# Two layers of linear attention and MLP on one core: the seven products of an MLP step in another order, with a planner that counts waits of a bank and the times of the DMA queue

## The chip, the cores and the metric

The kernel runs on one core of a Trainium2 chip. A core has five instruction streams that run side by side and meet through semaphores: TensorE (PE, matmuls and the weight loads ahead of them), VectorE (DVE), ScalarE (ACT), GpSimd (POOL) and SyncE (SP, which here issues every DMA). The metric is the device time of one execution, in microseconds (us); smaller is better. Before the change its median is 1041.44 us over three runs, from 1040.10 to 1042.91.

## What is computed

Two layers, each an attention block and an MLP block with a residual around each, on 2048 rows of 512 numbers:

```python
x = A_x
x = x + _A_ref(_layernorm(x, axis=-1), A_wqkv, A_w_phi, A_wo)
x = x + _B_ref(_layernorm(x, axis=-1), B_w1, B_w2)
x = x + _A_ref(_layernorm(x, axis=-1), A_wqkv, A_w_phi, A_wo)
x = x + _B_ref(_layernorm(x, axis=-1), B_w1, B_w2)
```

The attention block has 32 heads of 16. Queries and keys go through a learned 16x16 map per head and two softmaxes (of the result and of its negative, 32 features); the output is linear attention, `phi_q (phi_k^T V) / (phi_q phi_k^T 1)`, and a projection by `wo`. The MLP is `relu(x @ w1) @ w2` with 1792 hidden columns.

## The kernel before

**Numbers.** Every large matrix is held as a high and a low fp16 half, and a product is the sum of three matmuls (high by high, high by low, low by high). All of it accumulates in fp32 in PSUM.

**Stages.** The 2048 rows are 16 chunks of 128 rows. A first stage makes keys and values of all chunks and gathers `phi_k^T V` in two PSUM banks (`kv0`, `kv1`). The opening of a layer (`opening`, `summary`) turns these sums into the right-hand side `rhs` of the numerators (`pn`), brings chunks 0 and 1 through the back projection (`pw`) and computes the remaining queries (`pq`). Then the MLP runs over tiles of 256 rows (two chunks), each in 7 steps of 256 hidden columns; between the steps stand, as side work, the query features of later chunks (`look`), their numerators and back projection, and in layer 0 also keys, values and sums for layer 1.

**A step of the MLP.** In tiles 2 to 6 of layer 0 and 1 to 7 of layer 1, 84 steps in all, the 2x2 block product of a step is done in seven block products instead of eight (`hidden_by_seven`, PE line L1007). All seven go into one PSUM bank `ph` with four quarters of 128 columns, `at(0)` to `at(3)`. A running sum stands in `at(2)`: products 1, 6, 7 and 4 are added to it in this order, and after 1, 6 and 7 ACT copies it to SBUF (`snap`, L1019, tile `sn`). DVE then adds a copy to another quarter (`plus`, L1025): the first to product 2 in `at(0)`, the third to product 5 in `at(1)` giving `at(3)`, the second to `at(1)` once product 3 is there too. At the end ACT (L909) and DVE (L912) take the relu of the whole bank as two halves `h0` and `h1`, and the bank is free. Layer 0 has two banks for `ph`; in layer 1 `kv0` and `kv1` serve as well, so four take turns. The second half of the MLP (`mlp_out`, `py`, L1106) multiplies an earlier step's `h` by `w2`, in four pieces of three matmuls of 512 columns; LAG = 2 sets how many steps later.

**Which matmul is which in the profile.** `ph<-yT,w` is product 1 or 2, `ph<-wq_h,w` or `ph<-wq_l,w` product 4, `ph<-yT,s` product 3 or 7, `ph<-wq_h,s` or `ph<-wq_l,s` products 5 and 6 (`wq` holds sums of rows by then, `s` the sums of weights, loaded anew for each step by a DMA, L966). A product is 6 matmuls of 128 columns.

**What sets the order.** The order on each engine is made before the program is built. `add` records tasks with their engine, an assumed duration and what they read and write; `Plan.order` is a list scheduler that plays these through and issues whatever can start first. Block products and `py` pieces are moreover kept in the order of writing by `in_line`. Whoever reads or writes different quarters of a bank is independent for this planner. The framework that sets the semaphores, on the other hand, counts the whole bank: a product that is issued after a copy out of its bank waits for that copy, whatever quarter it writes, and a copy waits for the products issued before it. For a DMA the planner assumes a time in the queue and a landing (`t.kb` is its size). `NUDGES` is a table of numbers that shift tasks' ranks; ranks decide between tasks that could start at the same time.

**The order of a step before** (`steps_by_seven`; a dash marks products of the step ahead): 1, 4', 2, 3', side work, `py`, 6, 5, `py`, side work, 7, `py`, `py`.

## Time and profile before

| | before |
|---|---|
| device time, median of 3 (lowest, highest) | 1041.44 us (1040.10, 1042.91) |
| the profiled execution's own time | 1039.46 us |
| its span | 1037.7 us |
| PE busy | 992.8 us, 96% |
| DVE, ACT, POOL busy | 664.9, 495.3, 481.1 us |
| granted PE clock | 0.9 or more in 37 of 40 slices, 0.8 in the other three |

The span is the stretch between the first and the last instruction of one execution; the 1.8 us that the execution's time has more lie around it. Busy time of PE includes the drain of a matmul behind the last one of a run, so a short wait does not show as idle time. Rows of the timeline give the start of a run of equal instructions, its length, and in brackets the idle time before it with what ended it. PEld is the loading of the stationary operand, which runs ahead of the matmuls on the same instruction stream.

### The profile page before, as it was taken

What the parts mean: (1) busy time and instruction counts of PE and PEld (TensorE: products, weight loads), DVE (VectorE), ACT (ScalarE), POOL (GpSimd) and SP (SyncE); (2) the same over time, 40 slices, a digit from 0 to 9 for tenths busy, and PEclk for the clock granted to TensorE, in tenths of its full rate; (3) what the DMA queues carried; (4) which work ended last, traced back from release to release, by engine and by line L of the source; (5) the groups of instructions that cost most, each with busy time, mean ns of one, the idle gap of its engine ahead of it and who ended that gap; (6) DMA issues with size and microseconds to landing.
All of it is one profiled execution on the core that took longest, in us unless ns stands there. A gap on an engine that the chain in (4) does not pass through costs nothing.

```text
span 1037.7 us, 22144 instructions
## 1 busy us (share of the span) xinstructions
PE 992.8 (96%) x8930; PEld 626.5 (60%) x8930; DVE 664.9 (64%) x1391; ACT 495.3 (48%) x918; POOL 481.1 (46%) x389
## 2 busy tenths in 40 slices
PE   6999997899998999999999999999998999999998
PEld 5555554666665665657566664566665666676664
DVE  6778989884675867667565228987875444444332
ACT  7987875444534544435343215554554334333221
POOL 1379875479553645626342215357754323123000
PEclk9999998899999999999999999999999999999999
DMA  9576663466839383856743416674779384763531
GB/s 326 195 221 164 186 174 118 112 155 156 238 95 222 79 220 94 207 117 174 170 131 110 138 48 152 191 163 91 177 187 215 87 224 118 195 159 102 148 123 42
DMA packets 239143, 161.40 MB, mean 156 GB/s; under 512 B 178368, under 2 KB 185536, under 8 KB 239040
## 3 DMA queue, kind: packets, MB, share of 16 engines
q1 hardware_dynamic: 239040, 159.98, 59.3%
q8 instruction: 70, 1.15, 0.4%
q14 instruction: 33, 0.27, 0.1%
HBM read 88.64 MB, written 28.31 MB: 113 GB/s over the span
## 4 chain that ended last, share of the span: by engine, by line
PE 69%; DVE 12%; DMA 7%; ACT 5%; POOL 4%; issue 3%; SPq 1%; ACTq 0%; DVEq 0%; POOLq 0%
PE py L1106 22%; PE ph L1007 15%; PE pk L550 6%; PE ph L1075 6%; PE pw L550 6%; PE pv L550 5%; PE pq L550 5%; DMA pT<-p_q 2%; DMA yT<-n_b 2%; PE pn L802 2%; PE kv L688 2%; ACT sn L1019 1%; DMA xT<-n_a 1%; DVE fm_q L594 1%; DVE e_q L586 1%
## 5 line engine op out<-in xcount | busy, mean ns | idle before, releaser
L1106 PE MATMUL py<-w,h 128*128 128x512 f16 x1344 | 335.5, 380 | 0.0
L1106 PEld LDWEIGHTS <-h 128*128 128x128 f16 x1344 | 120.6, 98 | 97.8 <-issue 0.3
L1007 PEld LDWEIGHTS <-s 128*128 128x128 f16 x2016 | 129.9, 98 | 43.6 <-issue 9.7
L1019 ACT ACTIVATE sn<-ph 128x128 f32<-128x128 f32 x252 | 69.3, 275 | 177.2 <-PE ph L1007 172.6
L1025 DVE TENSOR_TENSOR ph<-ph,sn 128x128 f32<-128x128 f32 x252 | 70.9, 296 | 128.8 <-PE ph L1007 86.4
L550 PEld LDWEIGHTS <-xT 128*128 128x128 f16 x840 | 81.4, 98 | 95.8 <-issue 1.4
L912 DVE SCALAR_TENSOR_TENSOR h<-ph,h 128x512 f16<-128x512 f32 x112 | 76.1, 680 | 83.8 <-ACT h L909 83.8
L1007 PEld LDWEIGHTS <-w 128*128 128x128 f16 x1512 | 94.1, 98 | 38.5 <-issue 18.5
L909 ACT ACTIVATE h<-ph 128x512 f16<-128x512 f32 x112 | 66.3, 592 | 92.5 <-DVE ph L1025 63.0
L603 POOL TENSOR_TENSOR e_k<-e_k,fm_k 128x1024 f32<-128x1024 f32 x30 | 60.8, 2026 | 77.9 <-ACT fm_k L599 77.9
L1007 PE MATMUL ph<-yT,w 128*128 128x128 f16 x1008 | 83.3, 219 | 10.4 <-ACT sn L1019 6.4
L603 POOL TENSOR_TENSOR e_q<-e_q,fm_q 128x1024 f32<-128x1024 f32 x32 | 62.3, 1947 | 62.2 <-ACT fm_q L599 61.9
L1007 PE MATMUL ph<-yT,s 128*128 128x128 f16 x1008 | 83.9, 219 | 4.3 <-ACT sn L1019 2.9
L614 POOL TENSOR_TENSOR p_q<-e_q,p_q 128x1024 f16<-128x1024 f32 x32 | 71.5, 2237 | 35.0 <-ACT p_q L610 29.4
L550 PE MATMUL pw<-wo_h,oT 128*128 128x512 f16 x256 | 82.4, 384 | 2.2 <-DMA oT<-n_o 2.0
L550 PE MATMUL pv<-wv_h,xT 128*128 128x512 f16 x256 | 81.0, 379 | 0.7 <-DVE m_w L317 0.4
L550 PE MATMUL pk<-wk_h,xT 128*128 128x512 f16 x256 | 81.0, 379 | 0.1
L1075 PE MATMUL ph<-yT,w 128*128 128x256 f16 (+1 forms) x768 | 79.6, 264 | 0.2 <-DMA yT<-n_b 0.2
L469 POOL TENSOR_TENSOR n_o<-o,n_o 128x512 f16<-128x512 f32 x28 | 34.0, 1213 | 96.6 <-ACT n_o L466 96.6
L614 POOL TENSOR_TENSOR p_k<-e_k,p_k 128x1024 f16<-128x1024 f32 x30 | 68.3, 2276 | 20.3 <-ACT p_k L610 20.2
L1075 PEld LDWEIGHTS <-w 128*128 128x128 f16 x768 | 68.9, 100 | 9.8 <-issue 0.5
L550 PE MATMUL pq<-wq_h,xq 128*128 128x512 f16 x208 | 65.4, 379 | 0.4 <-ACT qs L711 0.4
(188 smaller groups left out, 1727.2 us busy)
## 6 DMA issues: line engine op xcount, KB each, us to landing
s<-s_dram SPq DMA_DIRECT2D x84, 512.0 KB, 4.0
q_dram<-qs SPq DMA_DIRECT2D x32, 256.0 KB, 3.1
ql<-q_dram SPq DMA_DIRECT2D x32, 256.0 KB, 3.3
xt_dram<-xT SPq DMA_DIRECT2D x26, 256.0 KB, 2.6
xq<-xt_dram SPq DMA_DIRECT2D x26, 256.0 KB, 3.1
xe<-in_A_x_dram SPq DMA_DIRECT2D x16, 256.0 KB, 5.7
x<-in_A_x_dram SPq DMA_DIRECT2D x16, 256.0 KB, 3.4
x_dram<-x SPq DMA_DIRECT2D x16, 256.0 KB, 2.7
```

Source lines behind the costliest of these rows:

```text
L469: add(POOL, 0.1 + n / 490, lambda: nc.gpsimd.tensor_sub(n16.at()[:, n:], src(), n16.at()[:, :n]), reads=[x], writes=[(n16, "l")])
L550: nc.tensor.matmul(pm.ap, xT.ap[:, a, k, :], W.ap[b][:, k, :], start=(k == 0 and i == 0), stop=(k == KC - 1 and i == 2))
L603: (nc.vector if fast else nc.gpsimd).tensor_tensor(e3, e3, sm.unsqueeze(2).to_broadcast([P, 2 * n, DH]), op=ALU.mult)
L614: (nc.vector if fast else nc.gpsimd).tensor_sub(p16.ap[:, 1, cols], ef, p16.ap[:, 0, cols])
L688: nc.tensor.matmul(o, k16.ap[:, a, g * P:(g + 1) * P], v.ap[:, b, g, :], start=(c == 0 and g % 4 == 0 and i == 0), stop=(c == NCH - 1 and ...
L909: nc.scalar.activation(h[0].ap, at(), AF.Relu)
L912: add(DVE, 0.62, lambda: nc.vector.scalar_tensor_tensor(h[1].ap, at(), 0.0, h[0].ap, op0=ALU.max, op1=ALU.subtract), reads=[ph, h[0]], wri ...
L1007: nc.tensor.matmul(at(r), weight_of(i, b, kk, s, summed), rows_of(y, i, a, kk), start=(first and kk == 0 and n == 0), stop=(kk == 1 and n ...
L1019: nc.scalar.activation(saved(i), at(2), AF.Copy)
L1025: add(DVE, 0.27, lambda: nc.vector.tensor_tensor(at(o), at(r), saved(i), op=ALU.add), reads=[(ph, r), (sn, i)], writes=[(ph, o)], boost=10 ...
L1075: nc.tensor.matmul(at()[:, j, cs.start * P:cs.stop * P], W1.at(b, k, slice(f * P, (f + 1) * P)), yT.ap[:, cs, a, k, :], stop=(k == KC - 1 ...
L1106: nc.tensor.matmul(py.ap, h[a].ap.rearrange("p j t -> p (j t)")[:, cols], W2.at(b, fs[j], slice(0, D)), start=(s == j == k == 0), stop=(s ...
```

## The change

The seven products are issued in another order. After the change a step reads: 1, 4', `py`, 3', 2', side work, 5, 6, `py`, side work, `py`, 7, `py`. Product 2 thus moves to the end of its step, behind product 3, and with it its `plus`; the two additions that end a step now stand one after the other ahead of the relu.

In the planner, a product now also depends on all earlier uses of its bank, the time assumed for a product is 0.336 instead of 0.34, and the queue of DMAs is modelled otherwise: a transfer takes its size by 190 or 250 KB per us in the queue (190 for a DMA transpose) instead of 1000 or 330. `NUDGES` is another table. So the order of nearly everything else moves as well; the operations themselves, their number and their sizes stay. Lines behind the table of nudges come two or three lines later in the changed file.

```diff
 NUDGES = (
-    (0, 995, (40000006, 40000018, 40000194, 40000198, 40000434, 40000986, 40001073, 40003344, 40003700, 40004317,
...
+    (0, 995, (10000087, 10000443, 10000979, 10001562, 10002629, 10003322, 10003862, 10004370, 10004598, 10005107,
...
             if t.engine == SP:
-                queue = max(t.end, queue) + t.kb / (1000 if t.turn else 330)
-                t.end = queue + (1.8 if t.turn else 2.2)
+                queue = max(start + (1.2 if t.turn else 0.85), queue) + t.kb / (190 if t.turn else 250)
+                t.end = queue + (0.45 if t.turn else 0.8)
...
-            in_line(add(PE, 0.34, go, reads=[op, *(W1.res if i in (1, 2, 4) else [summed])],
-                        makes=[ph] if first else [], writes=[] if first else [(ph, r)]))
+            in_line(add(PE, 0.336, go, reads=[op, *(W1.res if i in (1, 2, 4) else [summed])],
+                        makes=[ph] if first else [], writes=[] if first else [(ph, r)],
+                        after=[] if first else [u for u, _, _ in ph.uses]))
...
-        def second():
-            product(2, 0)
-            plus(0, 0, 0)
-
         def middle(i):
             product(i, 2)
             snap(i - 5)
-            if i == 7:
-                plus(3, 1, 2)
+
+        def fourth():
+            product(4, 2)
+            plus(3, 1, 2)
 
         def last():
             product(3, 1)
+            product(2, 0)
             plus(1, 1, 1)
+            plus(0, 0, 0)
             activate(ph, h)
 
-        return [first, second, partial(product, 5, 1), partial(middle, 6), partial(middle, 7), partial(product, 4, 2), last]
+        return [first, partial(middle, 6), partial(product, 5, 1), partial(middle, 7), fourth, last]
...
-        first, second, fifth, sixth, seventh, c21, c12 = hidden_by_seven(l, t, s)
+        first, sixth, fifth, seventh, fourth, last = hidden_by_seven(l, t, s)
...
         first()
         if ends:
             ends.pop(0)()
-        second()
+        do(0)
         if ends:
             ends.pop(0)()
         [f() for f in sides[0]]
-        do(0)
+        fifth()
         sixth()
-        fifth()
         do(1)
         [f() for f in sides[1]]
+        do(2)
         seventh()
-        do(2)
         do(3)
         [f() for f in sides[2]]
-        ends.extend((c21, c12))
+        ends.append(fourth)
+        ends.append(last)
         behind.append((t, s))
```

How the order moves is shown at three places. The first is PE in tile 7 of layer 1, where a step has no side work. Each row is the first matmul of a block product or of a piece of `py`; the brackets name the engine whose semaphore it waits for. Before:

```order
L1007 MATMUL ph_1_7_4_13504<-yT_1_7_12757,w1_0_135 128x128 [waits PE_49]
...
L1007 MATMUL ph_1_7_3_13432<-wq_l_103,w1_2_137 128x128 [waits DVE_49]
...
L1007 MATMUL ph_1_7_4_13504<-yT_1_7_12757,w1_2_137 128x128 [waits Activation_49]
...
L1007 MATMUL ph_1_7_3_13432<-yT_1_7_12757,s_1_7_3_13326 128x128
...
L1106 MATMUL py_1_14_13462<-w2_0_140,h0_1_7_1_13402 128x512
...
L1007 MATMUL ph_1_7_4_13504<-wq_l_103,s_1_7_4_13394 128x128 [waits DVE_49]
...
L1106 MATMUL py_1_14_13462<-w2_4_144,h0_1_7_1_13402 128x512
...
L1007 MATMUL ph_1_7_4_13504<-yT_1_7_12757,s_1_7_4_13394 128x128 [waits Activation_49]
...
L1106 MATMUL py_1_15_13495<-w2_0_140,h0_1_7_1_13402 128x512
...
L1106 MATMUL py_1_15_13495<-w2_4_144,h0_1_7_1_13402 128x512
```

And after the change, one step further on, again on PE:

```order
L1009 MATMUL ph_1_7_5_13564<-yT_1_7_12760,w1_0_135 128x128 [waits PE_49]
...
L1009 MATMUL ph_1_7_4_13496<-wq_l_103,w1_2_137 128x128 [waits DVE_49]
...
L1109 MATMUL py_1_14_13441<-w2_1_141,h0_1_7_2_13474 128x512
...
L1009 MATMUL ph_1_7_4_13496<-yT_1_7_12760,s_1_7_4_13386 128x128
...
L1009 MATMUL ph_1_7_4_13496<-yT_1_7_12760,w1_2_137 128x128
...
L1009 MATMUL ph_1_7_5_13564<-wq_l_103,s_1_7_5_13459 128x128 [waits Activation_49]
...
L1109 MATMUL py_1_14_13441<-w2_4_144,h0_1_7_2_13474 128x512
...
L1109 MATMUL py_1_15_13481<-w2_1_141,h0_1_7_2_13474 128x512
...
L1009 MATMUL ph_1_7_5_13564<-yT_1_7_12760,s_1_7_5_13459 128x128 [waits Activation_49]
...
L1109 MATMUL py_1_15_13481<-w2_4_144,h0_1_7_2_13474 128x512
```

Before, one product (4') stands between product 1, which is copied, and product 2, which waits for the copy; now 4', a `py` piece, 3' and 2' stand between product 1 and the next product of its bank. Between 6 and 7 there are two `py` pieces instead of product 5 and one, and between 7 and 4' one `py` piece and product 1 instead of two pieces and product 1.

The second place is where a bank comes free, on PE in tile 5 of layer 0 after the change, with two banks taking turns. The first row is product 2 of step 1, the last of its bank; the last but one row is the weight load of product 1 of step 3, which goes into the same bank and waits for DVE's `h1`:

```order
L1009 MATMUL ph_0_5_1_6186<-yT_0_5_5297,w1_2_137 128x128
...
L1009 MATMUL ph_0_5_2_6263<-wq_l_103,s_0_5_2_6081 128x128 [waits Activation_49]
...
L1109 MATMUL py_0_8_5584<-w2_6_146,h0_0_4_6_6126 128x512
...
L1109 MATMUL py_0_9_5631<-w2_3_143,h0_0_4_6_6126 128x512
...
L1009 MATMUL ph_0_5_2_6263<-yT_0_5_5297,s_0_5_2_6081 128x128 [waits Activation_49]
...
L1109 MATMUL py_0_9_5631<-w2_6_146,h0_0_4_6_6126 128x512
...
L1009 LDWEIGHTS w1_0_135 [waits DVE_49]
L1009 MATMUL ph_0_5_3_6342<-yT_0_5_5297,w1_0_135 128x128 [waits PE_49]
```

Three products and three `py` pieces stand between; before, the last product of a bank was 3', and a fourth `py` piece stood there as well.

The third place is ACT in the opening of layer 0, where the high halves of `rhs` are written (two rows), around them a piece of the sums of weights and the factors `fm` by which POOL multiplies the query features. Before:

```order
L943 ACTIVATE sums_0_h_2107<-sums_0_1854,s_w1_128 128x1024 [waits DMAHW1_49,DMAHW6_49,DMAHW0_49,Pool_49]
L742 ACTIVATE rhs0_0_2115<-rhsf0_0_2104 128x272 [waits DVE_49]
L742 ACTIVATE rhs0_0_2115<-rhsf1_0_2110 128x272 [waits DVE_49]
L711 ACTIVATE qs_0_14_2133<-pq_0_14_2089 128x512 [waits DMAHW5_49,PE_49,Activation_49]
L599 ACTIVATE fm_q0_3_1997<-fm_q0_3_1997 128x64
L599 ACTIVATE fm_q0_2_1972<-fm_q0_2_1972 128x64 [waits DVE_49]
```

And after the change:

```order
L744 ACTIVATE rhs0_0_2098<-rhsf0_0_2090 128x272 [waits DVE_49]
L744 ACTIVATE rhs0_0_2098<-rhsf1_0_2095 128x272 [waits DVE_49]
L945 ACTIVATE sums_0_h_2109<-sums_0_1984,s_w1_128 128x1024 [waits DMAHW5_49,DMAHW2_49,Pool_49]
L601 ACTIVATE fm_q0_2_1955<-fm_q0_2_1955 128x64 [waits DVE_49]
```

The sum piece and the factors now stand behind `rhs`, and the factor of chunk 3 has moved far back. On PE the last query product of this stage (`pq` of chunk 15) stood ahead of the first four `pn` and now stands behind them.

More of the change, by code (lines that the diff above doesn't have):

```diff
@@ L49 @@
 NUDGES = (
-    (0, 995, (40000006, 40000018, 40000194, 40000198, 40000434, 40000986, 40001073, 40003344, 40003700, 40004317,
-              40005127, 40005367, 40006801, 40007170, 40007814, 40010876, 40011402, 40011562, 40014708, 40037644,
-              40038018, 40039157)),
-    (995, 3940, (40015576, 40015600, 40015732, 40015800, 40016155, 40016335, 40018433, 40019189, 40019421, 40019857,
-                 40020982, 40021971, 40022108, 40022980)),
-    (0, 3940, (40023320, 40024941, 40029108)),
[8 rows of a table added]
 )
```

7 rows, old and new, of the table NUDGES are left out of this document.

## The prediction

> **What bounds the kernel now.** I read the page first, then the waits of PE and of its weight loads, then the timeline of an MLP step, then the steps with long waits. From the page:
>
> ```profile
> span 1037.7 us, 22144 instructions
> PE 992.8 (96%) x8930; PEld 626.5 (60%) x8930; DVE 664.9 (64%) x1391; ACT 495.3 (48%) x918; POOL 481.1 (46%) x389
> ```
>
> PE is the bound, and the matmuls stay the same. So the only thing to win is time in which PE could issue and does not. The waits of the weight loads (one row) and of PE (five), with us in total, times and the longest:
>
> ```profile
> PEld L1007 <- issue: 28.2, 80, 2.2
> ...
> PE ph L1007 <- ACT sn L1019: 9.2, 9, 2.1
> PE pn L802 <- DVE rhs L746: 4.4, 2, 2.9
> PE ph L1007 <- DVE ph L1025: 3.1, 6, 1.3
> PE pn L802 <- DMA pT<-p_q: 2.4, 3, 1.4
> PE pw L550 <- DMA oT<-n_o: 2.0, 4, 1.3
> ```
>
> PE's own rows show 12.3 us at L1007 in 15 waits, the weight loads 28.2 in 80. The loads tell more, because a short wait of a matmul hides in the drain of the one before. A step of layer 1 without side work shows it:
>
> ```profile
> 1009.26 0.50 PE L1007 MATMUL ph<-yT,w 128*128 128x128 f16 x6
> 1009.59 0.50 PE L1007 MATMUL ph<-wq_l,w 128*128 128x128 f16 x6
> 1009.85 0.28 ACT L1019 ACTIVATE sn<-ph 128x128 f32<-128x128 f32 x1 [1.41 <-PE ph L1007]
> 1010.18 0.50 PE L1007 MATMUL ph<-yT,w 128*128 128x128 f16 x6
> 1010.51 0.50 PE L1007 MATMUL ph<-yT,s 128*128 128x128 f16 x6
> 1010.85 0.81 PE L1106 MATMUL py<-w,h 128*128 128x512 f16 x3
> 1011.50 0.83 PE L1007 MATMUL ph<-wq_l,s 128*128 128x128 f16 x12
> 1012.01 0.69 DVE L912 SCALAR_TENSOR_TENSOR h<-ph,h 128x512 f16<-128x512 f32 x1 [0.66 <-ACT h L909]
> ...
> 1012.81 0.50 PE L1007 MATMUL ph<-yT,s 128*128 128x128 f16 x6
> 1013.35 0.28 ACT L1019 ACTIVATE sn<-ph 128x128 f32<-128x128 f32 x1 [0.71 <-PE ph L1007]
> 1013.66 0.30 DVE L1025 TENSOR_TENSOR ph<-ph,sn 128x128 f32<-128x128 f32 x1 [0.95 <-ACT sn L1019]
> 1014.44 0.50 PE L1007 MATMUL ph<-yT,w 128*128 128x128 f16 x6
> ```
>
> A product is issued in 0.336 (1010.18 to 1010.51) and drains 0.16 more; a piece of py takes 0.65 (1010.85 to 1011.50). Product 4 could end its issue at 1009.93, yet product 2 starts at 1010.18, 0.05 after the copy: 0.25 lost, and no row calls it idle. Going through the spacing of all 3528 matmuls of L1007, I find 88 starts that came over 0.04 late behind a copy or an addition, 30.4 us in sum, which is what the weight loads' 28.2 say too. They fall into three groups. Fifty-five are of the kind above, 0.19 to 0.29 each, 13.0 together; the first and the last:
>
> ```profile
> 325.65 0.50 PE L1007 MATMUL ph<-wq_h,w 128*128 128x128 f16 x6
> 326.24 0.49 PE L1007 MATMUL ph<-yT,w 128*128 128x128 f16 x6
> ...
> 1019.97 0.50 PE L1007 MATMUL ph<-wq_l,w 128*128 128x128 f16 x6
> 1020.56 0.50 PE L1007 MATMUL ph<-yT,w 128*128 128x128 f16 x6
> ```
>
> Fifteen are the visible ones, 12.3 and 15 drains of 0.16: 14.7. Eighteen small ones make the other 2.7. About half of the 30.4, 15.8, lies in layer 1. A large one looks like this:
>
> ```profile
> 782.61 1.25 SPq L480 DMA_TRANSPOSE yT<-n_b  x1
> ...
> 786.51 0.50 PE L1007 MATMUL ph<-wq_h,w 128*128 128x128 f16 x6
> 787.95 0.42 ACT L466 ACTIVATE n_u<-xn_b 128x256 f16<-128x256 f32 x1 [2.41 <-DMA yT<-n_b]
> 788.27 0.26 ACT L1019 ACTIVATE sn<-ph 128x128 f32<-128x128 f32 x1
> 788.58 0.49 PE L1007 MATMUL ph<-yT,w 128*128 128x128 f16 x6 [1.58 <-ACT sn L1019]
> ```
>
> ACT stood behind an instruction that waited for a transfer, and the copy behind it came 1.7 late.
>
> **The change part by part.** *Copies.* From the end of a product's issue to the first matmul that its copy releases the idle path is 0.59 (1009.59 to 1010.18). The new order puts at least 4', one py and 3', 2' there after product 1 (1.66), two py after product 6 (1.30), one py and product 1 after product 7 (0.98). The group of 55 goes: -13.0. The eighteen go as well, -2.7, but 4' now needs copy and addition within 0.98 in 46 steps; the idle path is 0.86 (1013.15 to the addition's end at 1013.96, and 0.05), and thirteen pairs of the old order with the same cover lost 0.04 each on average: +1.7.
>
> *The large waits.* If ACT and DVE are as late as now, the nine behind copies (9.2 and 1.5 of drains) gain 1.32 of cover each where they stand behind product 1 (five) and 0.65 elsewhere (four), which leaves 2.8. Of the six behind additions (3.1 and 1.0), three of 0.62 vanish, one of 1.46 keeps 1.15, and two of 0.38 stand ahead of 4', which had 1.63 of cover and now has 0.98: 1.03 each. Left 3.2. So 14.7 becomes 6.0; bounds 0 and, if all come back elsewhere, 14.7. Since transfers get longer times in the plan, fewer might come back; I take 6.0.
>
> *A new one.* In 13 steps DVE's third addition is now issued behind 4' and ahead of 3', with 0.65 for a path of 0.55. DVE is busy 64%, with operations up to 1.21 as at 457.26 below. Between 0 and 13 times 0.6, nearest to the pairs that pass: +2.0.
>
> *The bank.* Product 2 is now last, and two additions follow, so bank to free bank gets longer and its cover shorter. In layer 1 four banks take turns and the cover is 11 or more. In layer 0 it is three products and three py, 2.95, in the barest steps, where it was 3.6. The idle path is 1.85 (end of 3' issue 1010.85 to 1012.70); the second addition adds 0.25. Busy, it is longer; the longest of the 35 steps of layer 0:
>
> ```profile
> 456.78 0.50 PE L1007 MATMUL ph<-yT,s 128*128 128x128 f16 x6
> 457.26 1.21 DVE L594 TENSOR_REDUCE fm_k<-e_k 128x64 f32<-128x1024 f32 x1
> ...
> 458.98 0.27 DVE L1025 TENSOR_TENSOR ph<-ph,sn 128x128 f32<-128x128 f32 x1
> 459.28 0.60 ACT L909 ACTIVATE h<-ph 128x512 f16<-128x512 f32 x1
> 461.11 0.68 DVE L912 SCALAR_TENSOR_TENSOR h<-ph,h 128x512 f16<-128x512 f32 x1
> ```
>
> That is 4.68 (457.11 to 461.79). Setting each step's path, and 0.25, against the cover that the new order gives the same step, nine steps overrun, by 5.6 in all. The bounds are 0 and 41 (a rival below); I take half of what the rows give, +3.0, as the steps with long paths are those whose side work the plan now sees differently.
>
> *The opening of layer 0.*
>
> ```profile
> 168.50 0.36 DVE L730 SCALAR_TENSOR_TENSOR rhsf<-kv,mask 128x256 f32<-128x256 f32 x1
> ...
> 170.81 4.02 POOL L603 TENSOR_TENSOR e_q<-e_q,fm_q 128x1024 f32<-128x1024 f32 x2 [6.30 <-ACT fm_q L599]
> 170.99 4.14 DVE L746 TENSOR_TENSOR rhs<-rhsf,rhs 128x272 f16<-128x272 f32 x2
> ```
>
> Two subtractions of 272 columns took 4.14 while POOL multiplied; each pn waited for one (4.4 in sum). Now the factors that let POOL start stand behind rhs on ACT, so the two should run first, in about 0.4 each as the 256 columns of L730 do. That gives up to 4.4 back, and 0.3 of drains. Against it, the last pq no longer stands ahead of the pn; if rhs came no sooner, PE would wait 2.6 more there, less the 1.5 that the transposes behind the pn now come late, by the spacing of the matmuls: +1.1. I take -2.0, between them. The Trainium skill (SBUF — State Buffer, SBUF: two separate sides) calls the port pair of DVE and GpSimd an exclusive lock that blocks the loser for a whole instruction. The two rows agree, 4.14 beside 4.02; by the rule alone this term is -4.7 and the sum 2.7 less, and without a lock it is 0.
>
> *The rest.* The waits for transfers (2.4 and 2.0) may go or double, the first stage is shuffled by the nudges: 0, with 3 either way.
>
> Sum: -13.0 - 2.7 + 1.7 - 14.7 + 6.0 + 2.0 + 3.0 - 2.0 = -19.7. From the profiled execution's 1039.46 this gives 1019.8. That execution lies 2.0 below the median of the runs, so I expect a median of 1022.
>
> **Rivals.** *The large waits come back elsewhere.* ACT and DVE stay in-order and the transfers stay as slow, so with all 14.7, the bank's 5.6 and no help in the opening the gain is 30.4 - 14.7 - 1.7 - 2.0 - 5.6 = 6.4: 1035. For it speaks that the one shown began with a transfer, 5.3 from issue to the end of ACT's wait, and not with a product; against it the covers, doubled and more.
>
> *Layer 0 is paced by others.* If in layer 0 PE only waits elsewhere, for transfers or features, then layer 1's 15.8 less some 2.8 of leftovers is all: 13, or 1028. Against it, PE has 96% busy and the waits named for transfers are small.
>
> *The bank becomes the bound.* In 23 steps of layer 0 the new cover is 2.95 to 3.7, 3.15 on average. If the path from product 2 to the free bank were as long in each as the longest above (4.93 with the second addition), product 1 would wait 1.78 each time: 41 instead of 3, and the kernel would take 1060. It decides from a mean path of 4.2, where the whole gain is gone. For it speaks that 14 of 35 paths are over 2.9 now; against it that only one is over 4.1, and by the spacing no product 1 comes late behind its bank today. The Trainium skill (Perfetto Trace Analysis, Optimization Strategy) says that the same gap repeating on the engine that should be saturated can mean too few buffers. By it the gaps of layer 0 would move to product 1 instead of going; today's trace does not bear that out, since the repeated gap is there with four banks as well.
>
> *Nothing measurable.* The nudged order loses in the first stage, the openings or the turn of the layers what the steps win; between 570 and 740 the spacing shows 3 us lost in all, so there is room to lose: 1041.
>
> **How the numbers follow.** Forecast 0.58 (own range 1011 to 1032), large waits back 0.15 (1035), layer 0 paced by others 0.10 (1028), all terms at their good ends 0.04 (1008), nothing 0.05, bank 0.08. Faster by over 0.3% (3 us, about what a measurement here can tell from no change): 0.58 + 0.15 + 0.10 + 0.04 = 0.87; same 0.05; slower 0.08. The range of 1010 to 1038 leaves out the last two, and some of the good end.
>
> **What would show it.** Right: the weight loads' row at L1009 (the new L1007) falls from 28.2 to 10 or less, and a step without side work in tile 7 of layer 1 takes 4.94 instead of 5.18 (1009.26 to 1014.44). The copies' rows on PE keep a few waits at other places. A late bank shows as L1009 waiting for DVE's h, L914. The opening shows in L748 taking 1 instead of 4.14. Wrong: a step of the same length, or PE's waits growing at pn, pw or pk by as much as they fall at the products.

## The result, and the profile after

The changed kernel takes 1004.85 us (median of four runs, 1003.69 to 1006.36) where the kernel before, run beside it, takes 1040.77 (1039.54 to 1042.91). The ratio is 0.9654 with a 95% interval of 0.9631 to 0.9676: 36 us faster. The forecast was 1022 with a range of 1010 to 1038, so the sign was right, the gain almost twice as large, and the time below the range.

The profiled execution of the changed kernel took 1006.36, 1.5 above its median, and spans 1004.6. From its page, the span and the busy times:

```profile
span 1004.6 us, 22149 instructions
PE 978.1 (97%) x8930; PEld 625.0 (62%) x8930; DVE 661.8 (66%) x1391; ACT 492.6 (49%) x918; POOL 475.7 (47%) x389
```

The waits of PE and of its weight loads, in us with count and longest:

```profile
PEld L1009 <- issue: 4.6, 11, 0.9
...
PE ph L1009 <- ACT sn L1022: 2.1, 3, 0.8
...
PE ph L1009 <- DVE ph L1028: 1.2, 3, 0.7
...
PE tr_b L497 <- ACT xn_b L530: 7.1, 2, 5.2
```

The row that carried the prediction fell from 28.2 in 80 waits to 4.6 in 11. By the spacing of all matmuls of L1009, late starts behind copies and additions cost 5.6 instead of 30.4. A bare step of layer 1 shows the covers at work; the timeline of tile 7, from one product 1 to the next (here and below, rows of weight loads and of engines that the text does not speak of are left out):

```profile
946.99 0.50 PE L1009 MATMUL ph<-yT,w 128*128 128x128 f16 x6
947.32 0.50 PE L1009 MATMUL ph<-wq_h,w 128*128 128x128 f16 x6
947.58 0.28 ACT L1022 ACTIVATE sn<-ph 128x128 f32<-128x128 f32 x1 [0.76 <-PE ph L1009]
947.66 0.81 PE L1109 MATMUL py<-w,h 128*128 128x512 f16 x3
948.30 0.50 PE L1009 MATMUL ph<-yT,s 128*128 128x128 f16 x6
948.64 0.50 PE L1009 MATMUL ph<-yT,w 128*128 128x128 f16 x6
948.97 0.83 PE L1009 MATMUL ph<-wq_h,s 128*128 128x128 f16 x12
...
951.92 0.50 PE L1009 MATMUL ph<-yT,w 128*128 128x128 f16 x6
```

Copy 1 starts at 947.58 and is done at 947.86; the next product of its bank, 5, is due at 948.97. A step takes 4.93 (946.99 to 951.92) instead of 5.18.

Where PE does more in the same time is seen in equal windows. Each row gives us, PE's busy time and matmuls, granted clock, DMA share and GB/s. Before, the end of the opening of layer 0 and the densest part of its steps:

```profile
118.00:195.00 77.00, 66.77 (x471) 0.91 0.55 153
...
293.00:568.00 275.00, 263.37 (x2597) 1.00 0.60 149
```

And after:

```profile
118.00:195.00 77.00, 68.24 (x559) 0.93 0.59 164
...
293.00:568.00 275.00, 273.51 (x2766) 1.00 0.66 157
```

The idle gaps of all matmuls against their usual spacing, summed by place (us; the stretches are cut at the times of each profile):

| | before | after |
|---|---|---|
| first stage, 0 to 118 | 7.5 | 9.1 |
| opening of layer 0, 118 to 195 | 17.2 | 12.7 |
| 195 to 293 | 2.2 | 1.9 |
| layer 0, steps with the most side work, 293 to 568 | 18.1 | 3.0 |
| 568 to 742 | 3.2 | 2.7 |
| layer 1, 742 to the end | 16.6 | 2.1 |

Layer 1 gave 14.5, the dense steps of layer 0 gave 15.1, the opening 4.5. The first stage gave nothing. What it has more after is in the transposes at the start of this execution: until 15.8 they come 0.213 apart instead of the usual 0.112 (32 of them; before, 12 until 9.4). In another execution of the changed kernel (h3 below) it is 18 of them, and the first stage has 7.3.

The opening, in the timeline after (compare 4.14 for L746 and PE's wait of 2.87 before):

```profile
167.75 1.07 DVE L748 TENSOR_TENSOR rhs<-rhsf,rhs 128x272 f16<-128x272 f32 x2
...
168.52 1.63 PE L804 MATMUL pn<-rhs,pT 128*128 128x68 f16 x47 [0.40 <-DVE rhs L748]
...
169.58 2.24 POOL L605 TENSOR_TENSOR e_q<-e_q,fm_q 128x1024 f32<-128x1024 f32 x1 [1.41 <-ACT fm_q L601]
```

Both subtractions are over before POOL starts its multiplication. Not all of the opening got better: the last row of the waits above, PE at the transposes `tr_b` of the layer norm that follows, is two waits of 7.6 together by the spacing, where before they were 4.7.

### The profile page after: what moved, and what is told of

Read it like the earlier page. It is cut to its first block, busy times and chain, and to the rows that moved or that the text cites. A ratio compares the mean times of both kernels' runs of the same rounds, so it can differ in the third digit from the quotient of the medians.

```text
span 1004.6 us, 22149 instructions
## 1 busy us (share of the span) xinstructions
PE 978.1 (97%) x8930; PEld 625.0 (62%) x8930; DVE 661.8 (66%) x1391; ACT 492.6 (49%) x918; POOL 475.7 (47%) x389
## 4 chain that ended last, share of the span: by engine, by line
PE 75%; DVE 12%; DMA 4%; POOL 4%; ACT 2%; issue 2%; POOLq 0%; DVEq 0%; ACTq 0%; SPq 0%
PE py L1109 23%; PE ph L1009 17%; PE pk L552 8%; PE pv L552 7%; PE pw L552 6%; PE pq L552 6%; PE ph L1078 4%; PE pn L804 2%; PE kv L690 2%; DVE e_q L588 2%; DMA pT<-p_q 1%; DVE e_q L587 1%; DVE fm_q L596 1%; DMA yT<-n_b 1%; POOL e_q L605 1%
## 5 line engine op out<-in xcount | busy, mean ns | idle before, releaser
L1028 DVE TENSOR_TENSOR ph<-ph,sn 128x128 f32<-128x128 f32 x252 | 75.0, 297 | 127.8 <-PE ph L1009 102.9
L1009 PEld LDWEIGHTS <-s 128*128 128x128 f16 x2016 | 130.0, 98 | 42.4 <-issue 3.0
L1009 PEld LDWEIGHTS <-w 128*128 128x128 f16 x1512 | 95.4, 98 | 21.5 <-issue 1.6
L605 POOL TENSOR_TENSOR e_k<-e_k,fm_k 128x1024 f32<-128x1024 f32 x30 | 58.6, 1952 | 94.8 <-ACT fm_k L601 94.7
L1009 PE MATMUL ph<-yT,s 128*128 128x128 f16 x1008 | 83.7, 219 | 0.6 <-ACT sn L1022 0.5
L1009 PE MATMUL ph<-yT,w 128*128 128x128 f16 x1008 | 83.7, 219 | 0.0
```

The lines of the kernel that those rows point to most:

```text
L605: (nc.vector if fast else nc.gpsimd).tensor_tensor(e3, e3, sm.unsqueeze(2).to_broadcast([P, 2 * n, DH]), op=ALU.mult)
L1009: nc.tensor.matmul(at(r), weight_of(i, b, kk, s, summed), rows_of(y, i, a, kk), start=(first and kk == 0 and n == 0), stop=(kk == 1 and n ...
L1028: add(DVE, 0.27, lambda: nc.vector.tensor_tensor(at(o), at(r), saved(i), op=ALU.add), reads=[(ph, r), (sn, i)], writes=[(ph, o)], boost=10 ...
```

## The experiments

Two theories stood against each other. **C**: the gain comes from the covers, that is from what stands between a copied product and the next product of its bank. **N, P, S**: it comes from how the rest was planned: the table of nudges (N), the planner's new numbers (P), the place of side work on ACT and DVE (S). For each kernel the table gives the time, the kernel before on the same chip, and what PE lost in the seven-product steps behind copies, additions and freed banks, by the spacing of the matmuls of one profiled execution: in waits of up to 0.3 us and above.

| kernel | us | before | lost, small | lost, large |
|---|---|---|---|---|
| before | 1040.8 | | 15.6 | 14.8 |
| changed | 1004.9 | 1040.8 | 1.3 | 4.3 |
| e1 before, no nudges | 1067.1 | 1038.5 | 14.9 | 19.0 |
| e2 changed, no nudges | 1050.7 | 1038.5 | 1.4 | 21.7 |
| e3 new order, old planner, no nudges | 1058.4 | 1038.5 | 2.1 | 24.3 |
| e4 old order, new planner, no nudges | 1108.2 | 1038.5 | 11.9 | 66.3 |
| f1 changed, product 2 early again | 1019.8 | 1040.3 | 14.1 | 6.5 |
| f2 before, product 2 late | 1031.5 | 1040.3 | 0.9 | 20.0 |
| f4 before, eight copies first | 1036.7 | 1040.3 | 16.4 | 5.3 |
| g1 before, whole new order of products | 1030.4 | 1039.6 | 2.9 | 14.6 |
| g2 g1 with the edits of f3 and f4 | 1026.0 | 1039.6 | 2.8 | 10.7 |
| h1 g2 with additions first | 1027.3 | 1041.5 | 2.6 | 11.2 |
| i1 changed, table's first row only | 1020.1 | 1038.3 | 0.8 | 13.3 |
| i2 changed, table's second row only | 1041.3 | 1038.3 | 0.9 | 17.4 |

### Order and planner apart, without nudges

The table of nudges is emptied in both kernels (e1, e2), and the two other parts of the change are crossed: e3 has the new order of products with the old planner, e4 the old order with the new planner.

```diff
-NUDGES = ( ... )
+NUDGES = ()
```

For e3, the planner's lines go back:

```diff
-                queue = max(start + (1.2 if t.turn else 0.85), queue) + t.kb / (190 if t.turn else 250)
-                t.end = queue + (0.45 if t.turn else 0.8)
+                queue = max(t.end, queue) + t.kb / (1000 if t.turn else 330)
+                t.end = queue + (1.8 if t.turn else 2.2)
...
-            in_line(add(PE, 0.336, go, ..., after=[] if first else [u for u, _, _ in ph.uses]))
+            in_line(add(PE, 0.34, go, ...))
```

> The kernel before with an empty table of nudges. Theory C (covers: the gain of 36 us comes from what stands between a copied product and the next product of its bank): the table only decides between tasks that could start together, so this kernel lies within 15 us above 1040.8, say at 1048, and the weight loads' row at the products' line stays near 28 us, because each step still has 4' alone behind product 1. Rival N (the new table carries a good part of the gain): the old table had been worth something of the same size, so this kernel is slower than the kernel before by 15 us or more. The run is also the base for the three kernels beside it.

> The changed kernel with an empty table of nudges: order and planner new. Theory C: faster than the kernel before without nudges by 25 to 36 us, with the weight loads' row at the products' line under 10 us. Rival N: faster by less than 15 us, because most of the 36 us between the two kernels lies in their tables.

> No nudges; the new order of the seven products, but the old planner (0.34 for a product, no wait of a bank, the old times of the DMA queue). Theory C, as my prediction split it: the 73 small and tiny waits go (15.7 less 1.7) and of the large ones half, so 18 to 28 us faster than the kernel before without nudges. Rival P (the planner's new numbers carry the gain, the order alone leaves ACT and DVE as late as they were): under 10 us faster; the large waits of the copies and of the bank (products' line waiting for DVE's h) show as rows of PE.

> No nudges; the old order of the seven products, but the new planner (0.336, a product depends on all earlier uses of its bank, the new times of the DMA queue). Theory C: the 55 small waits of 0.19 to 0.29 stay, since they follow from the order alone; only large waits behind transfers can go, so 0 to 8 us faster than the kernel before without nudges, and the weight loads' row at the products' line stays at 15 us or more. Rival P: 15 us faster or more.

e1 took 1067.1 (ratio to the kernel before 1.0267, 1.0241 to 1.0292), e2 1050.7 (1.0115, 1.0087 to 1.0142), e3 1058.4 (1.0193, 1.0172 to 1.0214), e4 1108.2 (1.0669, 1.0643 to 1.0696).

The old table had been worth 28.6 us, the new one some 46 (1050.7 to 1004.9; 48 by the ratios). Order and planner together are worth 16.4 without tables, the order alone 8.7. So C as it was put falls: of the 36 us about half, 17 to 20, lies between the two tables. The small waits do follow from the order alone, as C said (14.9 in e1, 2.1 in e3), but the large ones went up.

e4 was expected 0 to 8 faster than e1 and came out 41 slower. The waits of PE in e4 show where:

```profile
PE ph L1000 <- ACT sn L1013: 41.5, 73, 2.5
```

and a bare step of its timeline shows which:

```profile
1087.33 0.50 PE L1000 MATMUL ph<-wq_l,s 128*128 128x128 f16 x6
...
1087.86 0.28 ACT L1013 ACTIVATE sn<-ph 128x128 f32<-128x128 f32 x1
1088.19 0.49 PE L1000 MATMUL ph<-wq_l,s 128*128 128x128 f16 x6 [0.36 <-ACT sn L1013]
```

Product 6 is copied, and product 5 right behind it now waits for the copy. In the old order 5 stands directly behind 6; the old planner, for which 5 was independent of the copy, issued it first, and the copy then waited for both. The planner's new rule makes 5 depend on the copy and puts it behind. By the spacing, products 5 and 6 lose 40.7 behind copies in e4 and 1.5 in e1, which is nearly all of the 41 (the planner's other new numbers were not tried alone). The rule and the order belong together: in e2, with 5 ahead of 6, the same products lose 1.2.

### The place of product 2, in both plans

In the runs f, g1, g2, g4 and h the finished order of a kernel, all engines, is kept row by row, and only single rows are moved. So the plan and its table stay in force. The cuts of these edits are shortened to their moves. In f1 product 2 goes back in the changed kernel, in f2 it goes late in the kernel before.

```diff
-        for t in plan.order():
+        for t in edit(plan.order()):
...
+    # f1, for every step
+    move(done, tag[2, step], tag["copy", 0, step], fourth)
...
+    # f2, for every step
+    move(done, tag[2, step], tag[3, step])
+    move(done, tag["plus", 0, step], tag[2, step], tag["plus", 1, step])
```

(`move` puts a task right behind the last of those named after it.)

> The changed kernel, its finished order of all engines kept row by row, with one edit: product 2 goes back to behind 4' of its own step (behind the copy of product 1), as before the change. In 56 of the 84 steps only 4', 0.336, then covers the copy's path of 0.59; in the others side work or py stands there as well. Theory C (cover): 56 times 0.25 come back, 14 us, and up to 20 if ACT is late in some: about 1019 (1016 to 1025), with the weight loads' row at the products' line up by 14 or more. Rival N (the tables of nudges carry the gain, the place of product 2 matters little once side work is placed well): under 5 us.

> The kernel before, its finished order of all engines kept row by row, with one edit: product 2 of each step, with its addition, goes to the step's end behind product 3; no other row moves. The 62 products that stood behind a copy with 0.34 of cover and lost 20.2 us in the profiled execution then have 1.3 or more. Theory C: 16 to 20 us faster, 1019 to 1024, with the fifty covers of 0.65 (6 to 7 and others) and the waits behind additions left as they are. Rival N: 5 us or less, because ACT is late anyway and the next copy pays. Rival B (bank): the additions of product 2 lengthen the turn of the bank in layer 0, and the products' line waits for DVE's h; then layer 1 alone gains, 10 us or less.

f1 took 1019.75 (ratio 0.9803, 0.9784 to 0.9821): 14.9 slower than the changed kernel, where C had 14. Its weight loads wait again, by the waits of PEld:

```profile
PEld L1009 <- issue: 18.3, 65, 2.1
```

f2 took 1031.5 (0.9917, 0.9893 to 0.9942): 8.8 faster than the kernel before, half of C's 16 to 20. The small waits went (15.6 to 0.9), and the large ones grew from 14.8 to 20.0. A quarter of these is one wait; the timeline of f2 around it:

```profile
431.22 3.39 SPq L480 DMA_TRANSPOSE xT<-n_a  x1
...
440.04 0.63 ACT L466 ACTIVATE n_a<-xn_a 128x512 f16<-128x512 f32 x1 [6.53 <-DMA xT<-n_a]
...
441.06 0.27 ACT L1019 ACTIVATE sn<-ph 128x128 f32<-128x128 f32 x1
...
441.38 0.80 PE L1007 MATMUL ph<-yT,s 128*128 128x128 f16 x6 [5.21 <-ACT sn L1019]
```

With PE earlier the transpose came right behind another transfer; ACT waited 6.53 to overwrite its source, the copy stood behind ACT's write, and product 7 came 5.4 late. In the kernel before, the same transpose took 1.25 in the queue (at 430.79), ACT waited 1.82 and the wait cost PE 1.33. Not all of the difference is the queue: from its start to its landing the transpose took 8.74 instead of 6.72, which was the longest of the 26 already then. Of the 4.7 by which ACT's wait grew, 2.0 are this, 0.4 the later start, and 2.3 that ACT itself came to its write earlier (433.51 instead of 435.77). So the row of the plan that was right for the old times was wrong for the new ones.

### The opening and eight copies, in the plan before

f3 takes the change's order of `rhs` over; f4 puts eight writes that wait for a transfer behind the copies that stood behind them.

```diff
+    # f3
+    move(done, tag["sums", 0], tag["rhs", 0, 1])
+    move(done, factors, tag["rhs_low", 0, 1])
...
+    # f4: seven writes of n, one of p_q
+    for t in [ns[i] for i in (30, 32, 40, 45, 48, 82, 86)] + [hs[63]]:
+        move(done, t, next_copy_behind(t))
```

> The kernel before, its finished order kept, with two moves in the opening of layer 0: on ACT the piece of the sums of weights goes behind the two high halves of rhs, and on DVE the two subtractions of rhs go ahead of the reduction for the factors of chunk 2. So they run before POOL starts to multiply. Theory C: the two take 1.0 to 1.2 together instead of 4.14, and PE's two waits at pn (2.87 and 1.55) shrink to 0.5 in all: 3 to 4.5 us faster, 1035.5 to 1037.5. Rival (the wait moves on): the transposes and pw behind pn, or the query features that are now later, wait instead: within 1 us of the kernel before.

> The kernel before, its finished order kept, with eight moves on ACT: eight writes of a half-precision tile (seven n, one p_q) that wait 1.0 to 2.5 for the transfer that still reads the tile go behind the copy of a product that stood right behind them. These copies made PE lose 9.9 us in the profiled execution. Theory C: 7 to 10 us faster, 1031 to 1034, and the longest wait of PE at the products' line falls from 2.1 to about 1. Rival (they come back elsewhere): the tiles written later make their transfers and what reads them later, 3 us or less.

f3 took 1038.1 (0.9979, 0.9962 to 0.9996): 2.2 faster, half of what C had. Its timeline:

```profile
170.31 0.86 DVE L746 TENSOR_TENSOR rhs<-rhsf,rhs 128x272 f16<-128x272 f32 x2
...
172.44 4.80 POOL L603 TENSOR_TENSOR e_q<-e_q,fm_q 128x1024 f32<-128x1024 f32 x2 [6.44 <-ACT fm_q L599]
172.80 2.65 DVE L349 SCALAR_TENSOR_TENSOR w<-w,s_w,w 128x1024 f16<-128x1024 f32 x1
...
176.43 1.42 PE L495 MATMUL tr_o<-ident,o 128*128 128x128 f32 x4 [3.85 <-DVE dn L810]
```

The subtractions take 0.86 without POOL beside them, where they took 4.14 with it. That part of C holds. But now another operation of DVE, L349, stands beside POOL and takes 2.65 instead of its usual 1.27, the quotients come behind it, and PE waits 3.85 at the transposes. In the changed kernel no such row stands between `rhs` and the quotients.

f4 took 1036.7 (0.9969, 0.9956 to 0.9981): 3.7 faster, between the two theories. The large copies' waits went from 10.7 to 1.2, but PE's waits at `pn` for the transposes of `p_q` rose from 2.4 to:

```profile
PE pn L802 <- DMA pT<-p_q: 6.4, 5, 2.8
```

### The whole order in the plan before

g1 brings the products and `py` pieces of the kernel before into the change's order; g2 adds f3 and f4; h1 adds that the third addition stands on DVE right behind its copy; h2 adds that L349 goes behind the quotients.

```diff
+    # g1, besides f2, for every step
+    ahead(tag[5, step], tag[6, step])
+    ahead(py[2], tag[7, step])
+    move(done, py[0], fourth)
...
+    # h1, for every step
+    move(done, tag["plus", 2, step], tag["copy", 2, step])
...
+    # h2
+    move(done, low_half, fourth_quotient)
```

> The kernel before, its finished order of DVE, ACT, POOL and SP kept row by row (but for the additions of product 2), with the products and py pieces of each step put in the change's order: 1, 4', py, 3', 2', side work, 5, 6, py, side work, py, 7, py (where a py piece can't go ahead, it stays). Moving product 2 alone gave 8.8 us, not 16 to 20, and left 20.9 us lost behind copies and additions: 9.9 in six copies, 10.6 in sixteen additions. Theory C (covers alone): with 1.3 also between 6 and 7 the six copies gain 0.65 each and the additions go with 4' later: 16 to 22 us faster than the kernel before, 1018 to 1024. Theory S (the side work of ACT and DVE must be placed for the new order): the large waits stay at 15 us or more, and the kernel is 8 to 13 us faster, 1027 to 1032, hardly more than with product 2 alone.

> The same, together with the moves in the opening of layer 0 (2.2 us alone) and the eight writes put behind copies (3.7 us alone). If the three are additive, 5.9 us less than with the order of the products alone. Theory C: that would be 1013 to 1018, half way or more to the change's 1004.85. Theory S: the eight writes are no longer those that delay a copy once the products have moved, so 2 to 4 us less, and 1024 to 1029.

> As the kernel with all three edits in the kernel before (1026.0), and on DVE the third addition of each step goes right behind its copy in the order, ahead of the side work (statistics of rows, residual sums, features, quotients) that stood before it. In that kernel's profile twelve waits of over 0.3 behind additions cost 9.3 us and nine short ones 1.6, most of them at 4' with its cover of 0.98. Theory D (what the change's new plan has beyond its order of products is side work that no longer stands ahead of the additions and copies): 6 to 10 us faster than 1026, 1016 to 1020, with PE's wait at the products' line for DVE's additions under 2 us. Rival (the gain is not there: DVE has as much work as before and the side work now late stops PE at pn, pw or the next copies): 3 us or less.

> The same, and in the opening of layer 0 the low half of a piece of w1 goes on DVE behind the four quotients of the first numerators. With the edit of the opening alone, that low half took 2.65 for its usual 1.27 beside POOL's multiplication, and PE then waited 3.85 for the quotients behind it. Theory: the quotients start 2.6 earlier and PE waits 1.3 there: 2 to 2.6 us faster than without this move. Rival: the quotients are slow beside POOL too, or pw and the layer norm behind are late all the same: 1 us or less.

g1 took 1030.4 (0.9915, 0.9890 to 0.9940): 9.2 faster, hardly more than product 2 alone. That is S, not C: with the covers of the change in force, 14.6 of large waits stay. Twelve of the sixteen, 10.5 us, are now at additions, since side work stands ahead of the addition on DVE; one in g1's timeline:

```profile
759.41 1.21 DVE L585 TENSOR_TENSOR e_q<-ql,fm_q 128x512 f32<-128x512 f32 x1
760.54 1.64 DVE L586 TENSOR_TENSOR e_q<-fm_q,ql 128x512 f32<-128x512 f32 x1
762.10 0.29 DVE L1025 TENSOR_TENSOR ph<-ph,sn 128x128 f32<-128x128 f32 x1
...
762.44 0.50 PE L1007 MATMUL ph<-wq_l,w 128*128 128x128 f16 x6 [1.75 <-DVE ph L1025]
```

The side work is itself long here, and POOL is beside it (rows of 758.13 to 760.07 and 760.37 to 761.63). In the kernel before, these two lines have 64 such operations with two inputs in SBUF: 27 overlap POOL's rows by less than 0.1 and take 0.68 to 0.69 each, the other 37 take up to 2.62. The additions, which read PSUM, take 0.30 with POOL beside them as without. How much of the large waits comes from this was not measured.

g2 took 1026.0 (0.9879, 0.9852 to 0.9906): 4.4 less than g1, where the two edits alone gave 5.9.

h1 tested whether the gain lies in the additions' place. It took 1027.3 (0.9877, 0.9846 to 0.9909), no better than g2: the theory (D in its expectation) is not borne out. The edit did only part of its work. The large waits behind additions fell from 9.3 to 6.6, while waits on a freed bank rose from 0.4 to 3.1, and those at `pn` from 4.2 to 4.6; the waits of PE and of its loads in h1:

```profile
PE ph L1007 <- DVE ph L1025: 5.3, 8, 2.3
PE pn L802 <- DMA pT<-p_q: 4.6, 4, 1.9
...
PEld L1007 <- DVE h L912: 4.6, 6, 1.1
```

h2 took 1027.7 (0.9895, 0.9856 to 0.9935), nothing either: PE's loss at the transposes fell from 6.0 to 3.3, and at `pw` behind them it rose from 2.3 to 6.0.

### The bank

g3 gives the steps of layer 1 only the two banks of layer 0.

```diff
-        tag = ("h", "kv0", "h", "kv1")[s % 4] if l == 1 else "h"
+        tag = "h"
```

> The changed kernel, but the steps of layer 1 take turns with the two banks of layer 0 only, so 75 products wait for a freed bank instead of 33, 43 of them with 2.95 to 3.2 of cover. The order of layer 1 is planned anew, so its part of the table of nudges fits less. My prediction's row (idle path 1.85 and 0.25): no product waits over 0.1 for the bank, and the kernel loses only what the table loses in layer 1, 0 to 6 us. The rival of the bank (path of 4.2 and more): 1.2 or more in each of 40 steps, 48 us slower than the changed kernel; half of that from a path of 3.7.

It took 1005.1 (0.9673, 0.9652 to 0.9694), the same as the changed kernel. By its spacing two products lost 1.4 behind a freed bank, the other 73 nothing. In the plan of the changed kernel the rival of the bank is out, and with it my +3.0. It is not out for the order as such, as i2 below shows.

### The table's two rows

The table has a row for the tasks ahead of the first seven-product step and one for those from there on; i1 and i2 keep one each.

```diff
 NUDGES = (
     (0, 995, ...),
-    (995, 3940, ...),
 )
```

> The changed kernel with only the first row of its table of nudges, which shifts the tasks ahead of the first step of seven products; the steps are planned without nudges. Without any table the kernel took 1050.7, with both rows 1004.85. By the spacing of the matmuls the two profiles differ by 24 us up to 293 us (first stage, keys and values, opening, first tiles) and by 24 behind it. Theory T (the large waits in the steps go by the table's second row, place by place): some 22 us of the 46 come back, 1024 to 1031, with PE losing 15 us or more behind copies and additions. Rival (a good start is what counts, since all later transfers follow from it): under 1012.

> The changed kernel with only the second row of its table, which shifts the tasks of the steps of seven products. Theory T: the first stage and the opening lose their 24 us again; the second row was found for a plan that began otherwise, so it keeps only a part of its own 24: 1030 to 1050. Rival (the second row does its work whatever stands ahead): 1024 to 1030, with under 8 us lost behind copies and additions.

i1 took 1020.1 (0.9826, 0.9792 to 0.9859), i2 1041.3 (1.0022, 1.0001 to 1.0043). The first row alone is worth 30.6 of the 46, the second alone 9.4; together they give more than the sum. The first row does more than its own stretch: without a nudge in the steps, the steps of layer 0 between 293 and 568 lose 7.2 in i1, while e2 loses 17.1 there and i2 19.7. So neither theory is quite right. How a plan begins decides in part which waits its later steps meet, and here the second row pays fully only together with the first. In i2 the bank does cost: by the spacing eight products of layer 0 lose 8.5 behind a freed bank, and PE's longest row at the products is

```profile
PE ph L1004 <- DVE h L909: 7.1, 8, 1.6
```

### Looking for a faster version

In the changed kernel three copies still came 0.64 to 0.99 late behind writes that waited for a transfer. g4 puts these writes behind the copies; h4 also puts the third additions right behind their copies; h3 is the changed kernel again, on the same chip as h4.

```diff
+    for t in [ns[53], ns[69], hs[62]]:
+        move(done, t, next_copy_behind(t))
```

> The changed kernel, its finished order kept, with three moves on ACT: the three writes that waited for a transfer ahead of the three latest copies (0.64, 0.94 and 0.99 lost at PE) go behind these copies. Theory: the three waits shrink to nothing, and as with the eight such moves in the kernel before some two thirds come back elsewhere: 0.5 to 2.6 us faster than the changed kernel, 1002.5 to 1004.5. Rival: nothing, or slower by up to 1, as the tile for the next transposes is written later.

> The changed kernel once more, for comparison with the one behind it on the same chip: 1003 to 1006.

> The changed kernel, its finished order kept, with the three writes behind copies as before (1002.9) and the third additions right behind their copies on DVE. Its profile has 1.7 us in three long waits behind additions and 1.2 in ten short ones. Theory D: 1 to 3 us faster than the changed kernel, 1001 to 1003.5. Rival: side work that is later stops PE elsewhere: the same, or slower.

g4 took 1002.9 (0.9652, 0.9631 to 0.9674), by the ratio no different from the changed kernel's 0.9654. h3 took 1005.1 (five runs, 1004.1 to 1006.3; 0.9661, 0.9633 to 0.9688) and h4 1003.3 (five runs, 1002.2 to 1003.7; 0.9642, 0.9618 to 0.9665). The runs of h3 and h4 do not overlap, the intervals of their ratios do: some 1.8 us, within the 0.3% that I count as no change. So no gain over the changed kernel is shown, and the additions add nothing to g4.

## Why the prediction was right and wrong

**Right: the fifty-five, and the eighteen.** Their small waits were a matter of the order alone. f1 brings them back (14.1 lost in small waits, 14.9 in time), and in every kernel with the new order they are 0.8 to 2.9. The step of 4.93 instead of 5.18 and the weight loads' row under 10 came as said. The new wait of 4' at its cover of 0.98 was put at 1.7 and cost 2.1. (The cover of 1.66 behind product 1 holds 2' as well, which my list of it left out.)

**The step that failed: no term for the table.** I took the place of everything else as given, "if ACT and DVE are as late as now", and of the nudged order I said only that it might lose. The table was worth 28.6 us in the kernel before and 46 to 48 in the changed one; this difference of 17 to 20 is half of the gain. By the crossed runs the rest is order and planner, 16.4, and the order alone 8.7. In the old plan, row by row, the order gave 9.2 (g1). These shares are not independent: in the finished plan of the changed kernel, taking back product 2 alone costs 14.9 (f1). Neither table was tried with the other kernel, so whether the new one is worth more because the new order leaves it more to win, or was only found with more luck or effort, stays open.

In the terms of the sum the same miss of 17 us is spread over many, nearly all to one side: the transfers 4.0, the profiled execution 3.5, the bank 3.0, the opening 2.5, the large waits 1.7 and the new wait behind DVE 1.6. All but the profiled execution were sized by rows of the old plan, or put at nothing.

**The large waits** (14.7 to 6.0; measured 4.3). The number was near, its working was not. By it, the covers absorb what stays late. With the covers alone the large waits were 14.6 (g1) and 20.0 (f2), because a moved product also shifts what ACT, DVE and the transfers meet. The reason I gave for fewer coming back, longer transfers in the plan, is hardly borne out either. Without a table the new planner does shorten ACT's waits for transfers, from 63.3 (e3) to 35.6 (e2), but PE's large waits only go from 24.3 to 21.7. And in the changed kernel ACT waits more for transfers than before, 46.2 in 31 waits after 35.5 in 26; the longest rows before:

```profile
ACT n_u L466 <- DMA yT<-n_b: 7.2, 5, 2.4
ACT p_q L610 <- DMA pT<-p_q: 7.2, 4, 2.7
ACT n_o L466 <- DMA oT<-n_o: 6.4, 4, 2.4
```

and after:

```profile
ACT n_u L468 <- DMA yT<-n_b: 11.3, 6, 5.2
ACT n_a L468 <- DMA xT<-n_a: 6.9, 5, 1.7
ACT n_o L468 <- DMA oT<-n_o: 6.7, 6, 2.6
```

These waits lie elsewhere in the steps. Counting from the last matmul of a copied product, 20 copies of the kernel before start over 0.3 us later than the earliest ones, and 77 of the changed kernel; nearly all of the 77 fall under a cover. What makes the large waits few is that covers and places fit each other, which comes with the table: without it they are 21.7, with its first row alone 13.3. Which of its shifts do it stays open.

**The bank** (+3.0; measured 0) and **the new wait behind DVE** (+2.0; measured 0.4): I priced both by rows of a busy DVE in the old plan. What the bank costs goes by the plan: with the same order it is 0 in the changed kernel and 8.5 in i2.

**The opening** (-2.0; measured -4.5 between 118 and 195). Here I chose between -4.7 and +1.1, and the end that goes by the exclusive port was the right one: the waits at `pn` fell from 4.75 to 0.56 by the spacing. The rest of the -4.5 is a balance: matmuls at a lower granted clock cost 3.6 before and 2.3 after (the stretch has 0.91 and 0.93 on average; over the whole execution before, two of 40 slices show 0.8, not three), `tr_b` costs 2.9 more, and small waits went. f3 shows the cause at `pn`: 0.86 for the two without POOL beside, 4.14 with it. The Trainium skill (SBUF — State Buffer, SBUF: two separate sides) names operations of DVE with two SBUF inputs among those that the lock holds up; f3 agrees, with L349 at 2.65 for 1.27. The quotients, which read `pn` in PSUM, go on at their usual length beside POOL's 2.24 (169.58) in the changed kernel, which agrees too; its timeline:

```profile
170.14 0.25 DVE L814 RECIPROCAL dn<-dn 128x16 f32<-128x16 f32 x1
170.43 0.42 DVE L815 TENSOR_TENSOR o<-pn,dn 128x256 f32<-128x256 f32 x1
```

The +1.1 that I held against it did not come. f3 also shows that the move alone is worth 2.2, if DVE's next long operation then stands beside POOL instead.

**The waits for transfers and the first stage** (0, with 3 either way). In the changed kernel the waits at `pn` and `pw` between 293 and 568 are 0.4 by the spacing, before 4.4; the first stage gave nothing. I had no term for a gain at `pn` and `pw`; with the order alone it did not come (g1: 5.3), so I put it down to the rest of the plan.

**The profiled execution.** I added 2.0 because that of the kernel before lay below its median. That of the changed kernel lies 1.5 above, so 3.5 of the miss is that. The longer start of this execution (9.1 in the first stage, 7.3 in h3) is a difference of about that size.

The rival "all terms at their good ends", 1008 with a chance of 0.04, was the nearest, and even it was too slow: its ends were those of the copies, and no end was given to the transfers and the rest. "Large waits come back elsewhere", 0.15, is what happens without a new table: g1 at 1030 and f2 at 1032 lie between its 1035 and the forecast.

## What to carry to other kernels

A reorder in a planned kernel has two prices: that of the waits which repeat in every step, which can be counted by covers and held (15 us here), and that of the large, single waits, which belong to the whole plan and are dealt anew by any move. Where a table like the nudges is exchanged, give it a term of its own, sized by what the old one had bought (28.6 here); where it is not, expect the removed large waits to return in good part, as in f2, f4 and h1. A planner's rule and an order must be judged together: at the products that the rule holds back it cost some 39 us in the old order and 1.2 in the new.

## What was not expected of the hardware

A transpose of `xT`, 1.23 to 1.41 in the queue in all 26 rows of the kernel before, took 3.39 in f2, where it came 0.05 behind the end of a load's row and not 0.46 behind it. It landed 2.0 later after its start, and with ACT earlier at its write the wait became 6.53 on ACT and 5.4 on PE. Of the 59 transposes of the kernel before that start within 0.1 of another transfer's end, 40 take under 1.5, so nearness alone does not do it, and the cause inside the queue was not measured.

The start of an execution varies: in the profiles of the changed kernel the transposes come at twice their usual spacing until 15.8 in one and until 10.9 in another (h3), where the first record of the granted clock stands at 16.0 and 12.0.

Faster is later: in the changed kernel 77 copies start over 0.3 us late (54 us in sum), in the kernel before 20 (16 us), and PE loses a fifth as much. How late the helpers are says little of what they cost as long as the covers are not set beside it.
